# Gate and value weight clamps on GpSimd as one two-step operation, with the head of the output stage and the first loads in another order

## The chip, the cores and the metric

The kernel runs on one core of a Trainium2 chip. The metric is device time in microseconds (us) of one execution; a median of three runs is given. One more execution was profiled. In the profile PE is TensorE's matmuls and PEld its weight loads, DVE is VectorE, ACT is ScalarE, POOL is GpSimd and SP is SyncE, which here only issues transfers. A queue such as SPq is the engine's instruction stream.

## The reference

Three layers follow one another. The MLP's weights are double precision (64 bits) on the host.

```python
# 1. attention: batch 4, 8 heads, 576 positions, head size 64
scores = scale * np.matmul(q, k.transpose(0, 1, 3, 2))   # local mask in heads 0-3, strided in 4-7
attn = np.exp(scores - np.max(scores, axis=-1, keepdims=True))
x = np.matmul(attn / (np.sum(attn, axis=-1, keepdims=True) + 1e-09), v)   # -> (2304, 512)
# 2. soft mixture of experts: 8 experts of 4 slots
logits = x @ phi
slot_input = softmax_over_tokens(logits).T @ x
slot_out = [np.maximum(slot_input[e] @ w1[e], 0.0) @ w2[e] for e in range(8)]
x = softmax_over_slots(logits) @ slot_out
# 3. gated MLP: (2304, 512) -> (2304, 1536) -> (2304, 512)
g, val = x @ w_gate, x @ w_val
return (g * (1.0 / (1.0 + np.exp(-g))) * val) @ w_out
```

## The kernel before

**Attention** runs in 16 units of two batches and one head. Unit n computes the scores (`qk`), then for the unit before it the transposes (`tr`) and the product with the values (`pv`). Keys and queries of a unit come in one transfer into one of three buffers (`load_qk`), values in one into one of two (`load_v`), and each unit also issues two half loads of expert weights (`load_half`). All transfers are issued by SP in the order of the code, and a transfer waits until the one eight places before it has landed (`par`, a small one that ACT issues, counts as the first).

**The experts** follow (w1, then w2), then the **output stage**, on which most of the change lies. The last layer never forms its input: slot outputs are multiplied into the gate and value weights first. For each of 12 blocks f of hidden columns, `a_mm(f)` multiplies the slot outputs (`soT`) with the block's weights, `a_st(f)` brings the result into the form `St[f]`. Tokens come in five blocks (four of 512, one of 256). The list `seq` holds 60 steps (part p, token block, f): 11 in part 0, 21 in part 1 and 28 in part 2. Steps 8 to 10, 29 to 31 and the last six are half steps of 256 tokens. At step n the code emits

- `omm(n-3)`: the output products of step n-3 (LAG = 3), for every 128 tokens hh x woh, hh x wol and hl x woh (high and low parts). In a step that ends its part the three products go tile by tile, in other steps all hh products go first and the hl products behind them;
- what earlier steps put down for step n in `todo` (`flush(n)`);
- `gv(n)`: gate and value products on PE, then sg (SiLU, ACT), h = sg x value (DVE), hh = h rounded (ACT) and hl = h - hh (POOL). The buffers of h are two, so the h of step n waits for the hl of step n-2; those of hh and hl are four;
- parts of a weight conversion as far as the step's `room` goes, and perhaps the start of the next (`stage`).

**The conversion** turns 64-bit weights into fp32 on the chip. For a tile of 128x1024 it takes, for each half k: `mag` (ACT, the magnitude of the high word), `clamp`, `shift`, `low` and `sign` (DVE). Three tiles, g 0, g 1 and o 0, are converted earlier; 15 follow in the output stage: g 2 to g 11 (one for each f) and o 1 to o 5 (one for two f). An o tile is split into woh (ACT) and wol (POOL). The constant CLP says whose clamps go to POOL; for the others DVE clamps from SBUF into a PSUM bank `cv`. When the last part of a g tile is emitted in step n, a_mm comes at step n+1 and a_st at n+2. HEAD is a string that orders what stands ahead of step 0: a is a_mm, s is a_st, w are matmuls without use (`warm`), g starts the first conversion, p emits conversion parts.

Engines run their instructions in order, so what is emitted first on an engine holds up all that is behind it.

Of the kernel before, what the change touches and what calls it, by code (L numbers as in the profile page):

```python
# [10 lines left out]
F32R = mybir.dt.float32r  # L11
# [26 lines left out]
LAG = 3  # L38
CVC = 0.6
CLP = "o"  # L40
WTAIL = 4
# [14 lines left out]
START = (2, 1)  # L56
HEAD = "a0 w1 g w1 a1 p2 s0 w2 p3 s1"
WARM0 = 8
# [55 lines left out]
def build(ctx: ExitStack, tc: tile.TileContext, cst, phi, kq, vh, w1, w2, wgv, wo, out):  # L114
# [72 lines left out]
    def conv(kind, j, through=False):  # L187
# [13 lines left out]
        def clamp(k):  # L201
            if not through:
                DVE.tensor_scalar(out=d[k], in0=d[k], scalar1=MAG_LO, scalar2=MAG_HI, op0=ALU.max, op1=ALU.min)
                return
            if kind in CLP:
                POOL.tensor_scalar(out=d[k], in0=d[k], scalar1=MAG_LO, scalar2=MAG_HI, op0=ALU.max, op1=ALU.min)
                return
            bk[k] = bank("cv", 1).bitcast(I32)
            DVE.tensor_scalar(out=bk[k].bitcast(F32), in0=d[k], scalar1=MAG_LO, scalar2=MAG_HI, op0=ALU.max, op1=ALU.min)
# [274 lines left out]
    with tc.manual_schedule():  # L484
# [14 lines left out]
        DVE.tensor_scalar_max(loc[:, 5:6], loc[:, 3:4], 31.0)  # L499
        load_qk(0)  # L500
        load_v(0)
        load_qk(1)
        SP.dma_start(out=phi_t, in_=phi.rearrange("p (c s) -> p c s", c=4))
        load_half(WSCHED[0])
        load_v(1)
        load_qk(2)

# [142 lines left out]
        cs = mid.tile([128, 4, S], F32R, name="cs")  # L650
        cst2 = [xp.tile([96, 3, 4, 4, 32], F32R, name=f"cst2{q}") for q in range(2)]
        cfs = [xp.tile([96, 3, 128], F32, name=f"cf{q}") for q in range(2)]
# [36 lines left out]

        def c_tr(bp, b, hf):  # L690
            ps = bank("tr", 3)
            for k in range(3):
                PE.transpose(ps[:, 96 * k:96 * k + 96],
                             cst2[hf][:, k, 2 * bp + b].rearrange("p q s -> p (q s)").bitcast(F32),
                             ident[0:96, 0:96])
            DVE.tensor_copy(cs[:, 2 * bp + b, 288 * hf:288 * hf + 288], ps[:, 0:288])
# [51 lines left out]
        DVE.tensor_copy(soT, ps[:, 0:128].rearrange("p (k s) -> p k s", k=4))  # L748
        while ctr:
            fn, a = ctr.pop(0)  # L750
            fn(*a)

# [65 lines left out]
        def omm(p, bi, f):  # L818
# [24 lines left out]
            for t in T:  # L843
                if first:
                    ob[t] = [bank("o", 4) for _ in range(2 if end and t + 1 == len(T) else 1)]
                mm(t, (0, 1, 2) if last else (0, 1))
            if not last:
                for t in T:
                    mm(t, (2,))
# [37 lines left out]
        def stage(n):  # L887
            if queue and len(staged) < 2:
                kind, j = queue.pop(0)
                parts = conv(kind, j, True)  # L890
                z = 4 if kind in CLP else 2
                for _, fn, k in parts[:z]:
                    fn(k)
                staged.append((n + 1, kind, j, parts[z:]))

        def part(n):
# [3 lines left out]
            if not parts:  # L900
                staged.pop(0)
                load_g(fr, "g", NG)
                if kind == "g":
                    at(max(n + 1, LAG + 1), a_mm, j)
                    at(max(n + 2, LAG + 2), a_st, j)
                    at(max(n + 2, LAG + 2), ready.add, (kind, j))
                else:
# [10 lines left out]
        def force(n, key):  # L918
            while key not in ready:
# [3 lines left out]
                if not staged:  # L923
                    stage(n)
                part(n)

        split_hi(0)
        split_lo(0, 0)
        split_lo(0, 1)
        for step in HEAD.split():  # L930
# [7 lines left out]
            elif k == "p":  # L938
                for _ in range(a):
                    part(-1)  # L940
            else:
                warm(a)
# [50 lines left out]
```

## Time and profile before

| | |
|---|---|
| median of 3 runs | 352.49 us (352.02 to 353.14) |
| profiled execution | 352.35 us, of which the span of the profile is 350.5 us |
| busy in the span | PE 334.3, DVE 235.4, ACT 193.2, POOL 139.0 us |
| output stage | from the first gate product at 146.28 us to the end |
| granted TensorE clock | 1.00 of full speed in all stretches looked at |

Time outside the span (1.85 us) is start and end. Busy time says which engine is full; whether a wait of PE costs anything is read from the rows with a releaser in brackets, which give idle time ahead of an instruction and who ended it. A pair such as x2 is two instructions in one row with their common time.

### The profile page before, as it was taken

To read this page: it belongs to the slowest core of one execution; us is meant where nothing else is said; L and a number is where in the kernel's file an instruction comes from. 1 tells how busy PE (TensorE), PEld (TensorE's weight loads), DVE (VectorE), ACT (ScalarE), POOL (GpSimd) and SP (SyncE) were. 2 spreads that over 40 slices of the span, in tenths; PEclk is the share of its full clock that TensorE was granted. 3 is DMA by queue.
4 is the path that set the end of the run, shared out by engine and by line. 5 is a ranking of instruction groups with operands and counts; after the bars stand their busy time and mean duration, and the time that the engine had idled before them with its cause. 6 is when DMAs were issued, how large, how long until landed. Compare 5 with 4: busy or idle time off the path is not lost.

```text
span 350.5 us, 7424 instructions
## 1 busy us (share of the span) xinstructions
PE 334.3 (95%) x2854; PEld 247.8 (71%) x2854; DVE 235.4 (67%) x492; ACT 193.2 (55%) x460; POOL 139.0 (40%) x150
## 2 busy tenths in 40 slices
PE   7999999899999999889998999999989999999995
PEld 4888888697674432456876686776857788888884
DVE  4988888796551265769869889997878633243342
ACT  2998897977521032567746665655654544344441
POOL 2223322114100200248483965456667743443431
PEclk9999999999999999999999999999999999999999
DMA  7999999988899998840423444142100003030331
GB/s 283 412 409 408 408 410 408 409 354 288 301 389 337 412 406 339 330 152 2 131 110 120 142 166 171 48 165 76 73 2 2 0 10 111 0 120 3 121 120 60
DMA packets 20803, 71.93 MB, mean 205 GB/s; under 512 B 2336, under 2 KB 2720, under 8 KB 20768
## 3 DMA queue, kind: packets, MB, share of 16 engines
q1 hardware_dynamic: 20624, 71.45, 53.7%
q8 instruction: 22, 0.36, 0.4%
q14 instruction: 13, 0.11, 0.1%
q10 hardware_dynamic: 144, 0.01, 0.0%
HBM read 66.73 MB, written 4.72 MB: 204 GB/s over the span
## 4 chain that ended last, share of the span: by engine, by line
PE 70%; DVE 9%; DMA 6%; ACT 6%; POOL 5%; issue 3%; DVEq 0%; POOLq 0%; SPq 0%; ACTq 0%
PE o L830 31%; PE sc L283 5%; PE pv L722 5%; PE pv L316 4%; PE sc L631 4%; PE tr L300 4%; PE gv L803 3%; DMA v<-in_vh 3%; DVE h L810 3%; PE gv L804 3%; DMA k<-in_kq 2%; PE tr L335 2%; PE gv L783 2%; POOL hl L812 2%; DVE cv L221 2%
## 5 line engine op out<-in xcount | busy, mean ns | idle before, releaser
L812 POOL TENSOR_TENSOR hl<-h,hh 128x512 fp32r<-128x512 f32 (+1 forms) x60 | 72.3, 1207 | 91.3 <-ACT hh L811 91.2
L830 PE MATMUL o<-woh,hh 128*128 128x512 f32 (+1 forms) x222 | 86.4, 390 | 0.4 <-DVE acc L855 0.2
L830 PE MATMUL o<-wol,hh 128*128 128x512 f32 (+1 forms) x222 | 85.9, 389 | 0.0
L810 DVE TENSOR_TENSOR h<-gv,sg 128x512 f32<-128x512 f32 (+1 forms) x59 | 37.5, 636 | 56.0 <-ACT sg L809 36.7
L830 PE MATMUL o<-woh,hl 128*128 128x512 f32 (+1 forms) x222 | 66.6, 390 | 1.1 <-POOL hl L812 1.1
L811 ACT CAST hh<-h 128x512 fp32r<-128x512 f32 (+1 forms) x60 | 34.7, 578 | 55.0 <-DVE h L810 55.0
L830 PEld LDWEIGHTS o<-woh,hh 128*128 128x128 f32 x222 | 41.8, 188 | 10.7 <-ACT acc L855 0.7
L830 PEld LDWEIGHTS o<-woh,hl 128*128 128x128 f32 x222 | 41.4, 188 | 10.9 <-POOL hl L812 1.9
L830 PEld LDWEIGHTS o<-wol,hh 128*128 128x128 f32 x222 | 41.8, 188 | 8.8
L261 POOL COPY v<-v 32x390 f32<-32x390 f32 (+1 forms) x48 | 21.7, 484 | 62.8 <-DMA v<-in_vh 45.9
L809 ACT ACTIVATE sg<-gv 128x512 f32<-128x512 f32 (+1 forms) x60 | 33.4, 557 | 21.1 <-PE gv L803 20.3
L293 ACT ACTIVATE tmp<-tmp,mx 128x96 f32<-128x96 f32 x144 | 40.1, 368 | 7.6 <-DVE mx L288 7.5
L283 PE MATMUL sc<-k 64*64 64x96 f32 x576 | 28.3, 251 | 1.6 <-DMA k<-in_kq 1.6
L283 PEld LDWEIGHTS sc<-k 64*64 64x64 f32 x576 | 25.4, 137 | 4.2 <-issue 2.4
L803 PE MATMUL gv<-cs,St 128*128 128x512 f32 (+1 forms) x60 | 25.5, 425 | 0.8 <-DVE St L792 0.8
L301 ACT COPY tmp<-tr 96x384 f32<-96x384 f32 x48 | 19.7, 480 | 8.8 <-PE tr L300 8.6
L774 POOL TENSOR_TENSOR wol<-wo,woh 128x512 fp32r<-128x512 f32 x12 | 15.3, 1292 | 22.0 <-ACT woh L771 22.0
L316 PEld LDWEIGHTS pv<-v,tmp 96*64 96x64 f32 x576 | 19.8, 137 | 5.0 <-ACT tmp L301 4.1
L316 PE MATMUL pv<-v,tmp 96*64 96x65 f32 x576 | 22.3, 226 | 0.4 <-DMA v<-in_vh 0.2
L804 PE MATMUL gv<-cs,St 128*128 128x512 f32 (+1 forms) x59 | 22.1, 375 | 0.2 <-DVE h L810 0.2
L221 DVE SCALAR_TENSOR_TENSOR cv<-g,cv 128x512 int32<-128x512 int32 x30 | 20.8, 692 | 0.6
L300 PE MATMUL tr<-cst_t,tmp 128*96 128x128 f32 x144 | 19.7, 279 | 1.5 <-ACT xT L337 1.5
(158 smaller groups left out, 479.1 us busy)
## 6 DMA issues: line engine op xcount, KB each, us to landing
w<-in_w SPq DMA_DIRECT2D x56, 512.0 KB, 8.6
g<-in_wgv SPq DMA_DIRECT2D x10, 1024.0 KB, 4.8
k<-in_kq SPq DMA_DIRECT2D x16, 576.0 KB, 8.3
g<-in_wo SPq DMA_DIRECT2D x5, 1024.0 KB, 4.8
v<-in_vh SPq DMA_DIRECT2D x16, 292.5 KB, 6.6
out<-osb SPq DMA_DIRECT2D x17, 256.0 KB, 2.1
wx<-in_w SPq DMA_DIRECT2D x7, 512.0 KB, 5.5
w<-in_wgv SPq DMA_DIRECT2D x4, 512.0 KB, 7.7
```

The source lines that it names most:

```text
L221: DVE.scalar_tensor_tensor(out=bk[k], in0=v[k][:, :, 0], scalar=29, in1=bk[k], op0=ALU.logical_shift_right, op1=ALU.bitwise_or)
L283: PE.matmul(out=ps[h, W * (i - i0):W * (i - i0) + W], lhsT=q[h, 64 * i:64 * i + 64], rhs=k[h, c0:c0 + W], start=True, stop=True, skip_grou ...
L293: ACT.activation(out=e[:, i], in_=e[:, i], func=AF.Exp, scale=1.0, bias=mx[:, i:i + 1])
L300: PE.transpose(ps[0:W, 128 * j:128 * j + 128], e[:, 3 * t + j], ident)
L316: PE.matmul(out=ps[64 * b:64 * b + 64, 65 * (i - i0):65 * (i - i0) + 65], lhsT=attile[0:W, i, 64 * b:64 * b + 64], rhs=v[0:W, 65 * (NT * b ...
L803: PE.matmul(out=pg[:, 0:n], lhsT=St[f][:, 0:128], rhs=csf[:, t0:t0 + n], start=True, stop=True)
L804: PE.matmul(out=pvv[:, 0:n], lhsT=St[f][:, 128:256], rhs=csf[:, t0:t0 + n], start=True, stop=True)
L809: ACT.activation(out=sg[:, 0:n], in_=pg[:, 0:n], func=AF.Silu)
L810: DVE.tensor_tensor(out=h[:, 0:n], in0=pvv[:, 0:n], in1=sg[:, 0:n], op=ALU.mult)
L811: ACT.copy(hh[bi, f][:, 0:n], h[:, 0:n])
L812: POOL.tensor_tensor(out=hl[bi, f][:, 0:n], in0=h[:, 0:n], in1=hh[bi, f][:, 0:n].bitcast(F32), op=ALU.subtract)
L830: PE.matmul(out=o[:, 0:c], lhsT=(a, a, l)[i][:, 128 * t:128 * t + 128], rhs=(woh, wol, woh)[i][f][:, c * k:c * k + c], start=(first and i ...
```

## The change

Six edits.

1. CLP becomes "go": the clamps of the g tiles go to POOL as well, and `shift` then reads the clamped half from SBUF. Every POOL clamp is one `tensor_scalar` whose first step is the minimum and whose second is the maximum; before, the maximum came first.
2. `stage` no longer emits the clamps at once: half k is put down for step n+1+k, and DVE's parts may start at n+2. a_mm and a_st come one step later than before (n+2 and n+3).
3. HEAD is another string; `t` emits the last two transposes of the slot weights (`c_tr`), which stood ahead of it, with banks of the tag o, and `h` the split of o 0. The tiles `cst2` move to a pool that stays open for that.
4. The first conversion starts at step -2, so its first clamp is put down for step -1, which no step flushes: 29 POOL clamps are issued, not 30, and the first half of g 2 goes unclamped.
5. In the first output step (part 0, block 0) the hh products of all tiles go ahead of the hl products.
6. The first transfers are issued in another order.

```diff
-CLP = "o"
+CLP = "go"
-HEAD = "a0 w1 g w1 a1 p2 s0 w2 p3 s1"
+HEAD = "h g a0 t a1 t s0 w1 s1 p1 w1"
...
-                POOL.tensor_scalar(out=d[k], in0=d[k], scalar1=MAG_LO, scalar2=MAG_HI, op0=ALU.max, op1=ALU.min)
+                POOL.tensor_scalar(out=d[k], in0=d[k], scalar1=MAG_HI, scalar2=MAG_LO, op0=ALU.min, op1=ALU.max)
...
-        load_qk(0)
+        for u in range(2):
+            load_qk(u)
         load_v(0)
-        load_qk(1)
+        load_qk(2)
+        load_v(1)
         SP.dma_start(out=phi_t, in_=phi.rearrange("p (c s) -> p c s", c=4))
         load_half(WSCHED[0])
-        load_v(1)
-        load_qk(2)
...
-        cst2 = [xp.tile([96, 3, 4, 4, 32], F32R, name=f"cst2{q}") for q in range(2)]
+        cst2 = [mid.tile([96, 3, 4, 4, 32], F32R, name=f"cst2{q}") for q in range(2)]
...
-                mm(t, (0, 1, 2) if last else (0, 1))
-            if not last:
+                mm(t, (0, 1, 2) if last and (p or bi) else (0, 1))
+            if not last or not (p or bi):
...
-                for _, fn, k in parts[:z]:
-                    fn(k)
-                staged.append((n + 1, kind, j, parts[z:]))
+                for i, (_, fn, k) in enumerate(parts[:z]):
+                    if i < 2:
+                        fn(k)
+                    else:
+                        at(n + 1 + k, fn, k)
+                staged.append((n + 2, kind, j, parts[z:]))
...
-                    at(max(n + 1, LAG + 1), a_mm, j)
-                    at(max(n + 2, LAG + 2), a_st, j)
+                    at(max(n + 2, LAG + 1), a_mm, j)
+                    at(max(n + 3, LAG + 2), a_st, j)
```

On POOL, around steps 18 to 20 of the output stage, these instructions stand in a row before (L812 is hl, L869 adds into an output tile, L774 is wol; no clamp is near):

```order
L869 TENSOR_TENSOR acc_2227<-osb,acc_2227 128x512
L774 TENSOR_TENSOR wol_2218<-wo_2179,woh_2206 128x512
L774 TENSOR_TENSOR wol_2219<-wo_2179,woh_2207 128x512
L812 TENSOR_TENSOR hl<-h,hh 128x512 x4
L869 TENSOR_TENSOR acc_2231<-osb,acc_2231 128x512
```

And these now, with the same steps' hl at L809, the addition at L866 and the clamps at L206:

```order
L866 TENSOR_TENSOR acc_2217<-osb,acc_2217 128x512
L771 TENSOR_TENSOR wol_2208<-wo_2169,woh_2196 128x512
L771 TENSOR_TENSOR wol_2209<-wo_2169,woh_2197 128x512
L206 TENSOR_SCALAR wg_2168<-wg_2168 128x512
L809 TENSOR_TENSOR hl<-h,hh 128x512
L206 TENSOR_SCALAR wg_2168<-wg_2168 128x512
L206 TENSOR_SCALAR wg_58<-wg_58 128x512
L809 TENSOR_TENSOR hl<-h,hh 128x512
L206 TENSOR_SCALAR wg_58<-wg_58 128x512
L809 TENSOR_TENSOR hl<-h,hh 128x512 x2
L866 TENSOR_TENSOR acc_2221<-osb,acc_2221 128x512
```

Four clamps of two g tiles now stand between the hl of three steps, and each hl is behind one or two of them.

On DVE, from the first `soT` to the h of step 2, before (L209 is the clamp, L217 shift, L221 low, L225 sign, L792 the last part of a_st, L810 is h):

```order
L696 CAST cs<-tr 128x288 x2
L209 TENSOR_SCALAR cv<-wg_2177 128x512
L217 TENSOR_SCALAR cv<-cv 128x512
L792 TENSOR_TENSOR St_2188<-gv,St_2188 64x256
L221 SCALAR_TENSOR_TENSOR cv<-g,cv 128x512
L225 SCALAR_TENSOR_TENSOR wg_2177<-g,cv 128x512
L209 TENSOR_SCALAR cv<-wg_2177 128x512
L792 TENSOR_TENSOR St_2189<-o,St_2189 64x256
L810 TENSOR_TENSOR h<-gv,sg 128x512
L217 TENSOR_SCALAR cv<-cv 128x512
L810 TENSOR_TENSOR h<-o,sg 128x512
```

And now, with St at L789 and h at L807:

```order
L696 CAST cs<-o 128x288 x2
L789 TENSOR_TENSOR St_2178<-gv,St_2178 64x256
L789 TENSOR_TENSOR St_2179<-o,St_2179 64x256
L217 TENSOR_SCALAR cv<-wg_2167 128x512
L807 TENSOR_TENSOR h<-gv,sg 128x512
L221 SCALAR_TENSOR_TENSOR cv<-g,cv 128x512
L807 TENSOR_TENSOR h<-o,sg 128x512
```

The five conversion parts that stood ahead of the first h are down to one, and the two St follow one another.

On SP the first transfers of the program stand like this in the difference (- before, + now; k are keys and queries, v values, w weights):

```order
 L252 DMA k0_76<-in_kq 128x1152
+L252 DMA k1_77<-in_kq 128x1152
 L258 DMA v0_79<-in_vh 64x1170
-L252 DMA k1_77<-in_kq 128x1152
-L503 DMA phi_t_74<-in_phi 128x128
-L182 DMA w_122<-in_wgv 128x1024 x2
+L252 DMA k2_78<-in_kq 128x1152
 L258 DMA v1_80<-in_vh 64x1170
-L252 DMA k2_78<-in_kq 128x1152
+L505 DMA phi_t_74<-in_phi 128x128
+L182 DMA w_127<-in_wgv 128x1024 x2
```

The second and third keys stand ahead of the first weights.

## Rows read from the trace of the kernel before

**Rows 1.** The page's busy times: us, share of the span, instructions.

```profile
PE 334.3 (95%) x2854; PEld 247.8 (71%) x2854; DVE 235.4 (67%) x492; ACT 193.2 (55%) x460; POOL 139.0 (40%) x150
```

**Rows 2.** Windows: stretch, length, busy us (count) by engine, clock, DMA share, GB/s.

```profile
181.78:257.89 76.11, 73.26 (x338) 54.51 (x336) 67.36 (x107) 43.31 (x84) 44.13 (x35) 1.00 0.33 111
272.77:350.50 77.73, 73.96 (x343) 60.86 (x341) 29.00 (x49) 32.09 (x59) 31.78 (x27) 1.00 0.17 61
```

**Rows 3.** Timeline, gate products of two full steps: start, us, instruction.

```profile
282.33 0.40 PE L803 MATMUL gv<-cs,St 128*128 128x512 f32 x1
285.59 0.40 PE L803 MATMUL gv<-cs,St 128*128 128x512 f32 x1
```

**Rows 4.** PE's waits, 140 to 275 us: total us, times, longest.

```profile
PE gv L783 <- DVE wg L225: 4.1, 5, 1.4
PE o L830 <- POOL hl L812: 1.1, 2, 0.6
```

**Rows 5.** Timeline of the head, some of DVE's rows and PE's first output product.

```profile
145.79 0.43 DVE L792 TENSOR_TENSOR St<-gv,St 64x256 fp32r<-64x256 f32 x1
146.25 0.70 DVE L221 SCALAR_TENSOR_TENSOR cv<-g,cv 128x512 int32<-128x512 int32 x1
...
148.43 0.43 DVE L792 TENSOR_TENSOR St<-o,St 64x256 fp32r<-64x256 f32 x1
148.89 0.69 DVE L810 TENSOR_TENSOR h<-gv,sg 128x512 f32<-128x512 f32 x1
150.29 0.50 PE L830 MATMUL o<-woh,hh 128*128 128x512 f32 x1 [0.16 <-ACT hh L811]
```

**Rows 6.** Instructions of the two clamp lines: duration ns min/median/max.

```profile
L206 POOL TENSOR_SCALAR wo<-wo x10: 1912/1922/1927, 159.4 to 263.6; 128x512 f32<-128x512 f32 x10
L209 DVE TENSOR_SCALAR cv<-wg x20: 684/695/697, 144.3 to 268.1; 128x512 f32<-128x512 f32 x20
```

**Rows 7.** POOL's timeline, 158 to 259 us, one row of each kind.

```profile
158.13 1.30 POOL L812 TENSOR_TENSOR hl<-h,hh 128x512 fp32r<-128x512 f32 x1 [2.70 <-ACT hh L811]
...
180.42 1.42 POOL L812 TENSOR_TENSOR hl<-h,hh 128x256 fp32r<-128x256 f32 x2
...
194.59 3.80 POOL L206 TENSOR_SCALAR wo<-wo 128x512 f32<-128x512 f32 x2
...
199.59 2.55 POOL L812 TENSOR_TENSOR hl<-h,hh 128x512 fp32r<-128x512 f32 x2
...
207.82 1.29 POOL L869 TENSOR_TENSOR acc<-osb,acc 128x512 f32<-128x512 f32 x1
209.08 2.56 POOL L774 TENSOR_TENSOR wol<-wo,woh 128x512 fp32r<-128x512 f32 x2
...
258.37 0.74 POOL L812 TENSOR_TENSOR hl<-h,hh 128x256 fp32r<-128x256 f32 x1 [2.38 <-ACT hh L811]
```

**Rows 8.** PE's timeline: step 28's first output product, and the last a_mm wait.

```profile
253.52 0.39 PE L830 MATMUL o<-woh,hh 128*128 128x512 f32 x1
...
261.87 0.63 PE L783 MATMUL gv<-wg,soT 128*32 128x256 f32 x4 [1.41 <-DVE wg L225]
```

**Rows 9.** Timeline: scores of units 1 and 2, values product of unit 13.

```profile
8.27 1.70 PE L283 MATMUL sc<-k 64*64 64x96 f32 x36 [0.89 <-DMA k<-in_kq]
...
13.15 1.70 PE L283 MATMUL sc<-k 64*64 64x96 f32 x36 [0.73 <-DMA k<-in_kq]
...
80.27 1.94 PE L316 MATMUL pv<-v,tmp 96*64 96x65 f32 x36 [0.24 <-DMA v<-in_vh]
```

**Rows 10.** Chain that ended last, in order of time: two early pieces.

```profile
0.73 3.96 DMA par<-in_cst
4.71 8.31 DMA k<-in_kq
```

**Rows 11.** Windows (columns as in Rows 2): DMA share early and late in attention.

```profile
8.00:10.00 2.00, 1.73 (x37) 1.64 (x38) 1.97 (x9) 2.00 (x8) 0.00 (x0) 1.00 1.03 422
74.00:76.00 2.00, 2.00 (x51) 1.93 (x48) 1.44 (x6) 2.00 (x9) 0.32 (x1) 1.00 1.03 412
```

More of the change, by code (lines that the diff above doesn't have):

```diff
@@ L688, in c_soft, with c_tr @@
             ACT.copy(t4[:, :, 2:4, :], t4[:, :, 0:2, :].bitcast(F32))
-        def c_tr(bp, b, hf):
-            ps = bank("tr", 3)
+        def c_tr(bp, b, hf, bk=("tr", 3)):
+            ps = bank(*bk)
             for k in range(3):
@@ L748, in build @@
         DVE.tensor_copy(soT, ps[:, 0:128].rearrange("p (k s) -> p k s", k=4))
-        while ctr:
-            fn, a = ctr.pop(0)
-            fn(*a)
         es_x.close()
@@ L903, in part @@
                 if kind == "g":
-                    at(max(n + 1, LAG + 1), a_mm, j)
-                    at(max(n + 2, LAG + 2), a_st, j)
-                    at(max(n + 2, LAG + 2), ready.add, (kind, j))
+                    at(max(n + 2, LAG + 1), a_mm, j)
+                    at(max(n + 3, LAG + 2), a_st, j)
+                    at(max(n + 3, LAG + 2), ready.add, (kind, j))
                 else:
@@ L924, in force @@
                     stage(n)
+                    continue
                 part(n)
-        split_hi(0)
-        split_lo(0, 0)
-        split_lo(0, 1)
         for step in HEAD.split():
@@ L940, in build @@
                     part(-1)
+            elif k == "t":
+                fn, b = ctr.pop(0)
+                fn(*b, bk=("o", 4))
+            elif k == "h":
+                split_hi(0)
+                split_lo(0, 0)
+                split_lo(0, 1)
             else:
```

## The prediction

> **What bounds the kernel now.** I read the busy times first [rows 1]: PE is busy 334.3 us of the span, so only time in which PE waits can be won, and the next engine, DVE, has 235.4 us. The windows show where DVE is dense: from 181.78 to 257.89 us it is busy 67.36 of 76.11 us, POOL only 44.13; from 272.77 us on DVE is busy 29.00 of 77.73 us [rows 2]. In that last stretch gate products of full steps follow one another every 285.59 - 282.33 = 3.26 us [rows 3], with PE always at work, and no conversion is left; the change has nothing to win or lose there. So the conversions' stretch, about 146 to 272 us, decides. PE's waits there [rows 4] are few and name their cause: a_mm waited five times, 4.1 us in all, for the last conversion part of its tile on DVE, and the output product waited twice, 1.1 us, for hl on POOL. A sixth place is the head: St of step 0 ends on DVE at 145.79 + 0.43 = 146.22 us, but h of step 0 starts at 148.89 us [rows 5]; between them DVE does conversion parts and the other St, and PE's first output product, which needs that h rounded, starts at 150.29 us.
>
> **The change part by part.**
>
> *Clamps off DVE.* 20 clamps of 695 ns leave DVE [rows 6], 13.9 us. DVE is not what ends last by itself, so this is worth only what PE waited for it.
>
> *a_mm one step later.* The tile's last part then has a step of 3.26 us [rows 3] more, against waits of at most 1.4 us [rows 4]. The five waits go: -4.1 us. If DVE fell late by 2 us the cover would be gone and the waits would come back.
>
> *Head.* On DVE only the second St (0.43 us) and one shift (of the clamp's shape, about 0.7 us) stand between St of step 0 and h, where the stretch from 146.22 to 148.89 us stood. St itself comes a little sooner, since the conversion parts ahead of it are gone, but the two magnitudes on ACT now stand ahead of a_mm's copy. I get h at about 147.0 us, 1.9 us sooner. From there h, hh and SiLU of steps 0 to 2 alternate on DVE and ACT as before, and the first evacuations of the output banks stand behind the h of step 2 as before; each handoff gives a little back, and hl of step 3, which ended at 158.13 + 1.30 = 159.43 us [rows 7], should end at 157.8 us. I take -1.6 us for the head, between -0.6 and -2.2 us. That the first output step has its hl products last hides hl of step 0, one of the two hl waits (0.6 us); this is inside the head's number. The other (0.5 us) comes from two clamps in a row ahead of half steps and goes, since there clamps now stand singly.
>
> *Sum for PE if POOL keeps up:* 1.6 + 4.1 + 0.5 = 6.2 us, which is 352.35 - 6.2 = 346.15 us.
>
> *Clamps onto POOL.* This is the cost. 29 clamps instead of 10 at 1.922 us [rows 6] add 36.5 us to POOL's 139.0 us [rows 1], and nearly all of it between step 3 and step 31. Counted in the new order, POOL has in that stretch, from the end of hl 3 to the end of hl 31, 27 clamps, 22 full hl, 6 half hl, 8 wol and 3 additions. Back to back they take 1.90, 1.275, 0.71, 1.28 and 1.29 us (3.80, 2.55, 1.42 and 2.56 us for pairs) [rows 7]: 51.3 + 28.1 + 4.3 + 10.2 + 3.9 = 97.8 us. Before, the same stretch lasted until 258.37 + 0.74 = 259.11 us [rows 7], that is 99.7 us, and POOL had 8 clamps in it. So POOL goes from two thirds full to full: it alone needs what the whole stretch took, and with the removed waits PE wants it shorter.
>
> What saves most of the gain is that PE needs an hl only three steps later. With 2 us of idle POOL (it runs dry around steps 10 and 11, where no clamp is queued; I allow 0 to 4 us) hl 31 ends at 157.8 + 97.8 + 2 = 257.6 us. Step 28 is the tight one, since behind its hl only two clamps and three half hl are left: 2 x 1.90 + 3 x 0.71 = 5.9 us earlier, 251.7 us. Step 28 ends its part, so its third product needs hl, some 0.45 us into it; it can start at 251.25 us. Before it started at 253.52 us [rows 8], and unhindered it would start at 253.52 - 1.6 - 0.5 - 2.7 (four of the five a_mm waits, 4.1 - 1.41) = 248.7 us. So POOL takes back 2.5 us and leaves 2.3 us of gain at step 28. Behind it comes the fifth a_mm wait, 1.41 us [rows 8], which goes, and half steps in which POOL runs free again. Sum: 2.3 + 1.4 = 3.7 us, 352.35 - 3.7 = 348.65 us. The profiled execution lies 0.14 us under the median of the three, so I take 348.7 us.
>
> *The clamp's price in the new order* (minimum first) stands in no row. The same operation with maximum first took 1912 to 1927 ns, all ten [rows 6], and swapping two steps of equal kind gives no reason to differ, so I take 1.90 us back to back. From below, VectorE's 0.695 us for the same clamp [rows 6] is the nearest bound; from above two passes at a two-input hl's 1.30 us [rows 7], 2.6 us. In the trace one clamp costs POOL 2.8 times what DVE pays. The Trainium skill (GPSIMD Engine Reference, section 4.1 Engine selection) says that one-input work on GpSimd is roughly at line rate; by that rule the clamps would take about what VectorE takes, POOL would never hold PE, and the time would be that of the first rival. The ten measured clamps speak against it.
>
> *First loads.* The second key transfer made unit 1 wait 0.89 us, the third unit 2 another 0.73 us [rows 9]; the third was issued only at 4.71 us, when par had landed [rows 10]. It no longer stands eighth, so these 1.6 us go at first. But the transfer engines run at a share of 1.03 and 1.02 to 1.03 from 8 to 76 us [rows 11], 410 to 422 GB/s; the bytes ahead of the values of unit 13 are the same, and PE already waits for those at 80.27 us [rows 9]. What attention wins early it waits for there: I take 0, with -1.6 us as the other end if the wait there doesn't grow. A loss needs the first values to come late; they are needed only after the transposes of unit 0, some 3 us after unit 1's scores.
>
> *The rest.* The c_tr in the head cost PE the same as ahead of it. cst2 in another pool, the missing clamp (one clamp's time, counted) and the shift's other source (0.69 to 0.70 us either way) are taken at nothing.
>
> **The rivals.**
>
> *POOL does not hold PE.* For that the 25 clamps up to hl 28 must be 2.5 us shorter in all, 1.80 us each, or POOL idle by nothing and the head better. Then 346.2 us, or 344.6 us if the first loads' 1.6 us stay too. For it: POOL's slack is only misjudged by 2.5 in 94 us. Against: ten clamps within 15 ns of each other. Chance 0.18, of which 0.03 for work at line rate.
>
> *POOL slower, and the kernel with it.* Each 0.1 us on a clamp costs 2.5 us by step 28, all on the path. From 1.90 + 3.7/25 = 2.05 us per clamp the kernel is slower than before; at 2.6 us it is 0.7 x 25 = 17.5 us later, 366 us; at 2.2 us 356 us. For it: nothing shows the new order's price, and POOL has no reserve. Against: same steps, same shape. Chance 0.15.
>
> *Feedback eats the gain.* POOL waits for hh (ACT), which waits for h (DVE), and DVE now waits in its order for clamps on POOL; two h buffers tie h to the hl of two steps before. A clamp also needs its magnitude from ACT, behind hh and, at four o tiles, behind the copies for woh. If POOL loses 1 us more at each of these four tiles, 3.7 us are gone: 352.4 us. For it: before, POOL already waited 2.70 us for hh in front of hl 3 [rows 7]. Against: once POOL is behind, hh is there before POOL asks. Chance 0.15.
>
> **How the numbers follow.** The forecast above, POOL nearly full, has 0.52; its own range is 346.1 (no idle, best head) to 350.5 us (means of whole rows, 1.922 and 1.31 us, instead of back-to-back times: 1.9 us more). The range that should hold 8 in 10 reaches below to 345.0 us and above to 351.6 us; what is left out is the slower rival and a little of the others. This kernel's runs can tell about 0.3%, 1.06 us. Faster by more: 0.52 + 0.18 and 0.02 of the feedback case, 0.72. Within: 0.13. Slower: 0.15.
>
> **What would show it.** POOL's clamps: 29 at 1.92 us, POOL near 175 us busy in all, DVE near 221 us. The waits of a_mm for DVE gone or under 1 us. h of step 0 near 147 us, hl 3 ended near 157.8 us. From step 18 on POOL without idle time, and PE's waits on hl, or on an h that waited for POOL, 2 to 3 us in all. Step 28's first output product near 251 us; the last stretch as long as before. Values of unit 13 still near 80 us. I am wrong if the clamp is not 1.9 us, if POOL has idle time of more than 4 us in the stretch, or if the head or attention moves by more than 2 us.

## The result and the profile after

The changed kernel takes 348.70 us (median of 6 runs, 346.51 to 350.81). The kernel before, on the same chip, takes 352.59 us (6 runs, 352.02 to 354.01). The ratio is 0.9885, 95% interval 0.9843 to 0.9927. Forecast was 348.7 us. The number is right, but one of the steps that led to it is wrong by a factor of three: a price on GpSimd. A wait and a slower clock, which the forecast doesn't have, make up for that.

The page's busy times of the changed kernel (us, share of the span, instructions), to be read against [rows 1]:

```profile
PE 330.6 (96%) x2852; PEld 246.5 (71%) x2852; DVE 223.6 (65%) x472; ACT 192.7 (56%) x460; POOL 139.6 (40%) x169
```

DVE lost what the clamps cost there. But POOL, which got 19 clamps more, is busy as long as before, not 175 us. The instructions of the clamp line say why (the g tiles' are shown; duration ns min/median/max, first and last start):

```profile
L206 POOL TENSOR_SCALAR wg<-wg x19: 608/617/641, 143.4 to 247.0; 128x512 f32<-128x512 f32 x19
```

With the minimum first a clamp takes 0.617 us. With the maximum first it took 1.922 us [rows 6]. No wait of PE names POOL now: in 135 to 275 us its largest waits are these (total us, times, longest), to be read against [rows 4]:

```profile
PE gv L800 <- DVE St L789: 2.0, 1, 2.0
PE o L827 <- DVE acc L852: 1.6, 2, 0.9
PE o L827 <- DVE acc L858: 0.5, 1, 0.5
PE gv L801 <- DVE h L807: 0.4, 1, 0.4
```

The five a_mm waits for the last conversion part and both hl waits are gone. New is one wait of 2 us for St on DVE. PE's gate products show what it cost. In the timeline of the kernel before, those of steps 0, 13, 14, 15 and 37 are

```profile
146.28 0.50 PE L803 MATMUL gv<-cs,St 128*128 128x512 f32 x1 [0.40 <-DVE St L792]
...
187.81 0.58 PE L803 MATMUL gv<-cs,St 128*128 128x512 f32 x1
...
191.70 0.40 PE L803 MATMUL gv<-cs,St 128*128 128x512 f32 x1
...
194.97 0.40 PE L803 MATMUL gv<-cs,St 128*128 128x512 f32 x1
...
275.61 0.58 PE L803 MATMUL gv<-cs,St 128*128 128x512 f32 x1
```

and in the timeline of the changed kernel, with what ACT and DVE did ahead of step 14 (idle time and its releaser in brackets):

```profile
145.23 0.50 PE L800 MATMUL gv<-cs,St 128*128 128x512 f32 x1
...
183.25 0.50 PE L800 MATMUL gv<-cs,St 128*128 128x512 f32 x1
...
187.95 1.13 ACT L768 CAST woh<-wo 128x512 fp32r<-128x512 f32 x2
...
188.34 0.59 PE L787 MATMUL gv<-asb,cst_t 128*128 128x256 f32 x2
...
188.99 1.22 ACT L199 ACTIVATE wo<-g 128x512 f32<-128x512 f32 x2
...
190.12 0.35 ACT L788 CAST St<-gv 128x256 fp32r<-128x256 f32 x1
190.50 0.43 DVE L789 TENSOR_TENSOR St<-gv,St 64x256 fp32r<-64x256 f32 x1 [0.27 <-ACT St L788]
...
190.99 0.50 PE L800 MATMUL gv<-cs,St 128*128 128x512 f32 x1 [2.05 <-DVE St L789]
...
195.90 0.40 PE L800 MATMUL gv<-cs,St 128*128 128x512 f32 x1
...
272.11 0.39 PE L800 MATMUL gv<-cs,St 128*128 128x512 f32 x1
```

Subtract step by step. At step 13 the changed kernel is 187.81 - 183.25 = 4.56 us ahead, 1.05 us of it from ahead of step 0. At step 14 it is 0.71 us ahead, and at step 15 it is 195.90 - 194.97 = 0.93 us behind: two steps lose all that was won. By step 37 it is 3.50 us ahead again. Step 14 multiplies with St of g 4 (the fifth g tile, first used here). Its a_st, one step later by the change, comes in step 14 itself. PE has done its matmul (L787) by 188.9 us, but on ACT the copies for woh and the magnitudes of an o tile, 1.13 + 1.22 = 2.35 us, stand ahead of St.

Behind the wait the clock falls. Windows of the changed kernel (columns as in [rows 2]), the clock behind POOL's figures:

```profile
189.00:190.00 1.00, 0.00 (x0) 0.00 (x0) 0.97 (x2) 1.00 (x3) 1.00 (x2) 1.00 0.99 119
193.00:194.00 1.00, 1.00 (x4) 0.78 (x3) 0.96 (x2) 1.00 (x2) 0.36 (x1) 0.50 0.00 0
194.00:195.00 1.00, 1.00 (x4) 0.81 (x3) 0.93 (x2) 0.70 (x2) 1.00 (x2) 0.50 0.00 0
```

0.50 is the lower of the two levels, 1.2 GHz. Step 14 lasts 195.90 - 190.99 = 4.91 us where the kernel before took 3.27 us: 1.64 us more. Of the 0.93 + 4.56 = 5.49 us lost in the two steps the wait and the clock are 2.05 + 1.64 = 3.69. Another 1.2 us are waits of PE for banks in step 13 (0.45 us at 184.20 us for the bank that h reads, 0.75 us at 186.84 us for an accumulator, where the kernel before waited 0.20 us in all); the rest was not split.

In attention the scores of units 1 and 2 no longer wait for keys, as foreseen, but one of nine mask instructions on DVE takes 2.3 us where all nine of before took 0.26 to 0.27 us:

```profile
L509 DVE TENSOR_SCALAR ms<-cst_t,par x9: 257/259/2318, 8.0 to 9.8; 128x96 bf16<-128x96 f32 x9
```

### The profile page after: what moved, and what is told of

The parts are those of the page before. It is cut to its first block, busy times and chain, and to the rows that moved or that the text cites. A ratio compares the mean times of both kernels' runs of the same rounds, so it can differ in the third digit from the quotient of the medians.

```text
span 346.1 us, 7436 instructions
## 1 busy us (share of the span) xinstructions
PE 330.6 (96%) x2852; PEld 246.5 (71%) x2852; DVE 223.6 (65%) x472; ACT 192.7 (56%) x460; POOL 139.6 (40%) x169
## 4 chain that ended last, share of the span: by engine, by line
PE 70%; DVE 12%; DMA 8%; ACT 6%; issue 2%; POOL 1%; SPq 0%; DVEq 0%; POOLq 0%
PE o L827 35%; DMA w<-in_w 5%; PE pv L722 4%; PE sc L631 4%; PE sc L283 4%; PE pv L316 3%; PE gv L800 3%; DMA v<-in_vh 3%; PE gv L801 3%; DVE h L807 3%; PE tr L300 2%; PE tr L335 2%; DVE cv L217 2%; ACT tmp L293 1%; PE tr L482 1%
## 5 line engine op out<-in xcount | busy, mean ns | idle before, releaser
L809 POOL TENSOR_TENSOR hl<-h,hh 128x512 fp32r<-128x512 f32 (+1 forms) x60 | 72.6, 1210 | 88.5 <-ACT hh L808 88.4
L807 DVE TENSOR_TENSOR h<-gv,sg 128x512 f32<-128x512 f32 (+1 forms) x59 | 37.5, 636 | 60.9 <-ACT sg L806 48.8
L261 POOL COPY v<-v 32x390 f32<-32x390 f32 (+1 forms) x48 | 23.7, 528 | 61.9 <-DMA v<-in_vh 54.8
L283 PEld LDWEIGHTS sc<-k 64*64 64x64 f32 x576 | 24.3, 133 | 4.4 <-DVE tmp L287 1.7
L221 DVE SCALAR_TENSOR_TENSOR cv<-g,cv 128x512 int32<-128x512 int32 x30 | 20.8, 694 | 0.8
```

What stands on the lines that cost most here:

```text
L261: POOL.tensor_copy(t4[0:W - 64, :, i0:i1, :], t4[64:W, :, i0 - 1:i1 - 1, :])
L283: PE.matmul(out=ps[h, W * (i - i0):W * (i - i0) + W], lhsT=q[h, 64 * i:64 * i + 64], rhs=k[h, c0:c0 + W], start=True, stop=True, skip_grou ...
L807: DVE.tensor_tensor(out=h[:, 0:n], in0=pvv[:, 0:n], in1=sg[:, 0:n], op=ALU.mult)
L809: POOL.tensor_tensor(out=hl[bi, f][:, 0:n], in0=h[:, 0:n], in1=hh[bi, f][:, 0:n].bitcast(F32), op=ALU.subtract)
```

## The experiments

Unless said otherwise each is the changed kernel with one edit. Ratios are against the kernel before on the same chip; kernels that ran on different chips are compared by ratio. Traces are compared by counting from the first gate product, because two executions of the same code don't reach it at the same time (145.23 and 145.90 us for the changed kernel). Theory: the two-step order sets the clamp's price, and step 14's wait with the clock behind it spends the difference. Rivals: the cheap clamp is the whole gain; POOL would have held PE as forecast; head or loads did it.

**The changed kernel again, beside the next three.** 

> The changed kernel once more, on the chip of the three below, to compare them with. Median 346.5 to 350.8 us as in its first six runs. If step 14 sits at the edge of a drop of TensorE's clock, its times spread more than those of the kernel before (over 1 us between lowest and highest) and follow the mean granted clock of the run.

348.74 us, ratio 0.9897 (0.9868 to 0.9927). Step 14's gate product waited 2.05 us again, and the next came 4.92 us later. Counted from the first gate product, every gate product up to that of step 37 comes within 0.1 us of its place in the first execution.

**Maximum first.**

```diff
-scalar1=MAG_HI, scalar2=MAG_LO, op0=ALU.min, op1=ALU.max
+scalar1=MAG_LO, scalar2=MAG_HI, op0=ALU.max, op1=ALU.min
```

> The changed kernel with the maximum first in each POOL clamp, nothing else. Theory A, the order of the two steps sets the price: all 29 clamps take 1.92 us instead of 0.62 us, POOL is busy about 177 us, the sum on record applies and POOL holds PE at step 28 by some 2.5 us on top of what step 14 loses, so 2 to 5 us slower than the changed kernel, 351 to 354 us. Theory B, something else made the clamps cheap (their tiles, their spacing): they stay near 0.62 us and the time stays that of the changed kernel.

349.52 us, ratio 0.9927 (0.9902 to 0.9952): about 0.8 us above the changed kernel beside it, with intervals that overlap. The 29 clamps take 1.92 us again, so the order of the two steps alone sets the price: that step of the prediction is refuted. POOL is now busy 175.1 us, the figure the prediction gave, and 58.55 of 60 us from 200 to 260 us; PE nowhere waits for hl. The wait for St in step 14 is there too, with a clock of 1.00 behind it in the profiled run:

```profile
192.79 0.50 PE L800 MATMUL gv<-cs,St 128*128 128x512 f32 x1 [2.06 <-DVE St L789]
196.12 0.39 PE L800 MATMUL gv<-cs,St 128*128 128x512 f32 x1
```

3.33 us to the next gate product here, 4.91 us in the changed kernel: the same wait with and without the fall. Counted from the first gate product, this execution is 1.59 us ahead of the changed kernel's second one at step 21, which is the clock, and only 0.79 us ahead at step 37: in the trace, too, the dear clamps cost 0.8 us here.

**g 4's a_mm and a_st one step sooner**, nothing else.

```diff
+                    e = 1 if j == 4 else 0
-                    at(max(n + 2, LAG + 1), a_mm, j)
-                    at(max(n + 3, LAG + 2), a_st, j)
-                    at(max(n + 3, LAG + 2), ready.add, (kind, j))
+                    at(max(n + 2 - e, LAG + 1), a_mm, j)
+                    at(max(n + 3 - e, LAG + 2), a_st, j)
+                    at(max(n + 3 - e, LAG + 2), ready.add, (kind, j))
```

> The changed kernel, but a_mm and a_st of tile g 4 alone come one step sooner, as before the change, so that St of g 4 isn't made in the very step that needs it. Theory A, this one tile costs 2.05 us of wait and then about 1.6 us by the lower clock: the wait of the gate product on St is gone, the granted clock is 1.00 in every stretch, and the time is 3 to 4.5 us lower, 344 to 345.5 us. Rival: PE waits there for DVE's evacuations and for h anyway; then the wait moves to a_mm of g 4 or to the next output product, and the time falls by less than 1 us.

345.66 us, ratio 0.9811 (0.9778 to 0.9843), 3.1 us under the changed kernel on the same chip. Its largest waits of PE in the same stretch:

```profile
PE o L827 <- DVE acc L852: 1.1, 2, 0.9
PE gv L780 <- DVE wg L225: 0.7, 1, 0.7
```

The wait for St is gone, the mean clock is 0.998 or more in all five runs, and 0.7 us of an a_mm wait is back. From the first gate product to that of step 37 it takes 269.91 - 146.60 = 123.31 us, the changed kernel run again 126.98 us: 3.67 us less, the 3.69 us of wait and clock. One tile's place was worth as much as nearly all that the change had won.

**Nine matmuls of no use ahead of step 14's gate product**, into the bank that it then overwrites. The wait stays, but PE is busy in it.

```diff
+            for _ in range(9 if (bi, f) == (0, 4) else 0):
+                PE.matmul(out=pg, lhsT=warm_t[:, 0:128], ...)
```

> The changed kernel with nine matmuls of no use (128x512) ahead of the gate product of step 14, where PE otherwise waits 2.05 us for St on DVE. They cost PE no time that it has work for, and keep it busy. Theory: the fall of the granted clock to the 1.2 GHz level behind the wait is what makes step 14 last 4.9 instead of 3.3 us; with PE busy the clock stays at 1.00, the next gate product comes 3.3 us later, and the time is 1.2 to 1.8 us under the changed kernel's 348.7, near 347.2 us. Rival: the clock falls for another reason or gives its time back later; then 348.4 to 349.2 us, no difference that can be told, and the clock in the stretch behind step 14 still shows 0.50.

347.38 us, ratio 0.9833 (0.9800 to 0.9866). In its timeline the matmuls fill the wait, and the next gate product comes 3.33 us later:

```profile
188.41 2.10 PE L801 MATMUL gv<-warm_t 128*128 128x512 bf16 x9
190.63 0.50 PE L802 MATMUL gv<-cs,St 128*128 128x512 f32 x1
...
193.96 0.40 PE L802 MATMUL gv<-cs,St 128*128 128x512 f32 x1
```

So with PE busy in the wait step 14 takes 3.33 us, and that part comes back without any of the work being done sooner. Within the spread of the two ratios the size is the 1.6 us read from the steps. The fall is not bound to the wait in every execution: the mean clock is under 0.996 in 22 of the 34 runs of kernels that have this wait (the changed kernel, it again, maximum first, old head, old loads), in 1 of 6 here, and in 1 of 22 of the four kernels that make g 4's St sooner. The kernel before, without that wait, has such runs as well, 14 of the 45 beside the experiments, so a mean clock doesn't say where the fall lay.

**Other pairs of steps on the clamps**, one execution, for the prices. Each tile has another pair; tiles without both bounds are not clamped on that side.

> A price list, not a race: on each of the 15 tiles the GpSimd clamp has another pair of steps (two instructions per tile, 128x512 fp32 each), among them both orders of minimum and maximum with the true bounds, one step alone (scalar2 absent), the same step twice, and a multiply by 1 or an add of 0 ahead of or behind one of them; tiles without both bounds go unclamped on one side. Theory A, the first step sets the price: every pair that begins with maximum takes about 1.92 us and every pair that begins with minimum 0.62 us, maximum alone too about 1.9 us or at least clearly above minimum alone. Theory B, it is the very pair maximum-then-minimum (one slow combination): only that pair takes 1.92 us, twice maximum, maximum and multiply, maximum and add take about 0.62 us. Theory C, 0.62 us is the exception (one fused minimum-maximum), all others take 1.9 us. The time of the whole kernel is of no interest; 347 to 350 us by any of them.

POOL's timeline of this kernel, one clamp each of g 2 (minimum, maximum), g 3 (maximum, minimum), o 1 (minimum alone), g 4 (maximum alone), o 3 (multiply, maximum) and o 4 (multiply, add):

```profile
144.98 0.62 POOL L218 TENSOR_SCALAR wg<-wg 128x512 f32<-128x512 f32 x1
...
158.75 1.91 POOL L218 TENSOR_SCALAR wg<-wg 128x512 f32<-128x512 f32 x1
...
163.36 1.48 POOL L218 TENSOR_SCALAR wo<-wo 128x512 f32<-128x512 f32 x1
...
166.07 1.48 POOL L218 TENSOR_SCALAR wg<-wg 128x512 f32<-128x512 f32 x1
...
193.59 1.93 POOL L218 TENSOR_SCALAR wo<-wo 128x512 f32<-128x512 f32 x1
...
231.07 0.62 POOL L218 TENSOR_SCALAR wo<-wo 128x512 f32<-128x512 f32 x1
```

The single run took 349.08 us. Theories A and B fall, and C holds with one addition: minimum-maximum and multiply-add take 0.62 us, the nine other pairs tried 1.91 to 1.94 us, and one step alone 1.48 us, more than those two pairs of two steps. How GpSimd carries them out is not seen.

**Minimum first in the kernel before**, ten clamps, nothing else changed.

> The kernel before with nothing changed but the order of the two steps in its ten GpSimd clamps, minimum first. Theory: each of the ten takes 0.62 instead of 1.92 us, GpSimd's busy time falls by 13 us to about 126 us, and since PE waited for hl only twice, 1.1 us in all, of which one wait lies behind a pair of these clamps, the time falls by 0.4 to 0.6 us: 352.0 us where the kernel before has 352.5, hardly to be told. Rival: the cheap clamp is itself most of what the change gains; then 349 to 350 us.

352.49 us, ratio 0.9991 (0.9971 to 1.0011). POOL's busy time falls to 126.1 us, one of its two hl waits (0.6 us) is left, and the five a_mm waits are still 4.1 us. The cheap clamp by itself is worth nothing that can be told: from the first gate product to that of step 37 the profiled execution takes 129.32 us, the kernel before 129.33 us. (Its clock stood at 0.50 from 153 to 156 us; step 3 came 1.48 us later than before, and by step 11 that was made good.) The later a_mm with the clamps left on DVE was not tried, so what their leaving DVE is worth by itself is not shown.

**Maximum first, with g 4 one step sooner.** Here the prediction's account of POOL can be tested, since step 14 no longer hides it.

> The version with g 4's block product one step sooner (345.7 us) and the clamps with the maximum first, at 1.92 us each. The prediction's account of GpSimd then holds as it was worked out: hl 31 can't end before about 257.2 us, step 28's third product is held, and some 2 to 3 us of waits for hl appear between steps 18 and 28: 347.7 to 348.7 us. Rival: the account is too strict, since with the changed kernel the dearer clamps cost 0.8 us though GpSimd was busy 58.6 of 60 us; then 345.5 to 346.7 us, and PE waits on hl under 0.7 us.

347.42 us, ratio 0.9839 (0.9805 to 0.9872): 0.0028 above the version with cheap clamps, about 1.0 us by the ratios, whose intervals overlap. The traces say more. Here are the first gate product and step 28's first output product, first in this version, then with cheap clamps:

```profile
145.01 0.50 PE L800 MATMUL gv<-cs,St 128*128 128x512 f32 x1
...
250.21 0.40 PE L827 MATMUL o<-woh,hh 128*128 128x512 f32 x1
```

```profile
146.60 0.50 PE L800 MATMUL gv<-cs,St 128*128 128x512 f32 x1
...
249.46 0.40 PE L827 MATMUL o<-woh,hh 128*128 128x512 f32 x1
```

That is 105.20 us against 102.86 us: by step 28 the dear clamps cost 2.34 us, and 2.45 us by the last gate product. Up to step 17 the two agree to 0.06 us; 0.3 us go by step 18, 1.0 more by step 21 and 1.1 more by step 22. (In absolute times the cost is hidden, since this execution came to soT 1.59 us sooner.) Two waits of PE are new:

```profile
PE o L827 <- ACT osb L862: 0.9, 2, 0.7
PE o L827 <- POOL hl L809: 0.8, 1, 0.8
```

The second is the wait for hl that the prediction had. The longer one of the first row, ahead of step 22, also begins on POOL; its chain on DVE, ACT and PE is

```profile
214.19 0.69 DVE L217 TENSOR_SCALAR cv<-wg 128x512 int32<-128x512 int32 x1 [0.98 <-POOL wg L206]
214.79 0.68 DVE L807 TENSOR_TENSOR h<-gv,sg 128x512 f32<-128x512 f32 x1
215.56 0.62 ACT L808 CAST hh<-h 128x512 fp32r<-128x512 f32 x1 [4.06 <-DVE h L807]
216.09 0.58 ACT L862 COPY osb<-o 128x512 f32<-128x512 f32 x1
216.72 0.50 PE L827 MATMUL o<-woh,hh 128*128 128x512 f32 x1 [0.69 <-ACT osb L862]
```

A shift on DVE waits for a clamp on POOL, h stands behind the shift, hh waits for h, the copy that frees the output bank stands behind hh on ACT, and PE waits for the bank. This is the feedback that the prediction had as a rival. POOL's own time is as forecast:

```profile
155.66 1.30 POOL L809 TENSOR_TENSOR hl<-h,hh 128x512 fp32r<-128x512 f32 x1 [0.85 <-ACT hh L808]
...
255.02 1.48 POOL L809 TENSOR_TENSOR hl<-h,hh 128x256 fp32r<-128x256 f32 x2
```

hl 3 ends at 156.96 us, hl 31 at 256.50 us: 99.5 us, where the prediction had 97.8 + 2 = 99.8. So the theory's account holds in the trace; the median lies between the times of theory and rival.

**a_mm and a_st one step sooner for every tile**, by the rule of the kernel before (n+1 and n+2).

```diff
+                    e = 1
```

(in place of the condition on g 4)

> The changed kernel with the block product a_mm and the step a_st one step sooner for every tile, as in the kernel before (0.62 us clamps on GpSimd kept). Theory from the prediction's sum: the later a_mm is worth the 4.1 us of waits; the wait for St in step 14 goes as with g 4 alone, so against 345.7 us the waits of a_mm come back: 4 to 5 of them, 0.5 to 1.4 us each, 348 to 349.5 us. Rival: with 20 clamps off DVE the last conversion parts end in time by themselves; waits of a_mm under 1.5 us in all, 345.5 to 346.8 us, and the later a_mm brought nothing.

355.94 us, ratio 1.0087 (1.0058 to 1.0116): slower than the kernel before, and by the ratios some 10 us slower than with g 4 alone. Both theories fell short. The waits are five again, and longer:

```profile
PE gv L780 <- DVE wg L225: 5.6, 5, 1.9
```

Around the longest, that of g 5 ahead of the gate product of step 15, the clock falls as well:

```profile
194.97 0.63 PE L780 MATMUL gv<-wg,soT 128*32 128x256 f32 x4
197.47 1.07 PE L780 MATMUL gv<-wg,soT 128*32 128x256 f32 x4 [1.87 <-DVE wg L225]
198.46 0.80 PE L800 MATMUL gv<-cs,St 128*128 128x512 f32 x1
```

In the kernel before, g 5's a_mm comes behind the gate product of step 15 (194.97 us):

```profile
198.32 0.63 PE L783 MATMUL gv<-wg,soT 128*32 128x256 f32 x4
```

So the old rule is not the old place. With two clamps fewer on DVE the code emits g 5's last part one step sooner (step 14, before 15), and the old rule takes a_mm along to step 15; in the changed kernel it stands in step 16, as before the change. What kept g 5's wait away was a whole step between last part and a_mm. PE's waits for parts, accumulators and St sum to 8.5 us here and to 2.3 us with g 4 alone; the other 4 us, the slower clock among them, were not split.

**The head in its old order**, without the old string's five conversion parts (p2 and p3).

```diff
-HEAD = "h g a0 t a1 t s0 w1 s1 p1 w1"
+HEAD = "h t t a0 w1 g w1 a1 s0 w2 s1"
```

> The changed kernel with the head in the order of the kernel before (no conversion part ahead of step 0 save those that order emits, block products and warm matmuls in their old places, the last two transposes ahead of all). Theory from the prediction's sum: the head's order is worth 1.6 us at hl of step 3 and at the steps behind it up to step 13; but in the changed kernel the wait for St in step 14 swallows what comes early, so the time rises by less, 0 to 1 us: 348.7 to 349.7 us, with hl 3 ending near 158.5 to 159 us and a shorter wait for St in step 14. Rival: the head's gain is carried to the end; 350.3 us, the wait in step 14 still 2 us.

348.13 us, ratio 0.9866 (0.9835 to 0.9897), not slower than the changed kernel. hl 3 ends at 156.38 + 1.30 = 157.68 us. From the start of soT, the tile with which the head begins, to the end of hl 3 it is 15.76 us here, 15.68 us in the changed kernel (155.88 + 1.30 = 157.18 us), 17.58 us before [rows 7]. The three soT, before, changed and here:

```profile
141.85 0.29 DVE L748 COPY soT<-sc 128x128 f32<-128x128 f32 x1 [0.36 <-PE sc L746]
```

```profile
141.50 0.29 DVE L748 COPY soT<-sc 128x128 f32<-128x128 f32 x1 [0.36 <-PE sc L746]
```

```profile
141.92 0.29 DVE L748 COPY soT<-sc 128x128 f32<-128x128 f32 x1 [0.36 <-PE sc L746]
```

Both expectations fail: the order in the string, apart from the parts left out, brings nothing that can be told. In three of its runs the mean clock was 1.00 (346.74 to 347.86 us), in three 0.993 or 0.994 (348.41 to 349.73 us), about 1.9 us apart by the means, near the price of the fall; where it lay in these runs is not seen (the profiled one has none).

**The first loads in their old order.**

```diff
-        for u in range(2):
-            load_qk(u)
+        load_qk(0)
         load_v(0)
-        load_qk(2)
-        load_v(1)
+        load_qk(1)
...
+        load_v(1)
+        load_qk(2)
```

> The changed kernel with the first loads in the old order. Theory A: the new order brought the values copies and the memset on POOL onto the mask building of DVE, where one instruction of 96 columns took 2.3 us instead of 0.26; with the old order it takes 0.26 us again, the scores of unit 12 start near 61.7 instead of 62.6 us, attention ends 0.7 to 1 us sooner, and some of it arrives at the end: 0 to -1 us. Rival: the transfers set attention's end, the values of unit 13 come at 80.8 us as they do now, and nothing changes at the end.

347.93 us, ratio 0.9883 (0.9851 to 0.9915), within the spread of the changed kernel's 0.9897. The mask instructions are back at 0.26 to 0.27 us and the wait for St is still 2.1 us. The cost on DVE is shown in the trace, its worth in time isn't settled.

**g 4 sooner, and a memset on POOL moved** from attention's first microseconds to unit 3.

```diff
-        POOL.memset(eT, 0.0)
...
+        at_late(3, POOL.memset, eT, 0.0)
```

> The version with g 4's block product one step sooner (345.7 us), and GpSimd's memset of 10.65 us (for the transposed exponentials) moved from the first microseconds to unit 3. Theory: the mask instruction on DVE that lasts 2.32 us was blocked by GpSimd's row of copies and memset; without the memset it shortens to between 0.26 and about 1.3 us, unit 2's scores lose their 1.06 us wait, and the expert stage starts some 0.7 us sooner: 344.8 to 345.3 us. Rival: the transfers bound attention anyway and the values of unit 13 wait for the same bytes; then 345.4 to 346.0 us. A second rival: the copies alone block it just as long, and the mask instruction stays at 2.3 us.

344.49 us, ratio 0.9752 (0.9717 to 0.9788), the lowest of all kernels run. The long mask instruction is down to 0.56 us:

```profile
L509 DVE TENSOR_SCALAR ms<-cst_t,par x9: 257/257/561, 8.1 to 10.1; 128x96 bf16<-128x96 f32 x9
```

So the memset (1.05 us at 10.65 us in the changed kernel, behind 1.33 us of copies) made up most of it; the copies alone, still there, add 0.3 us. The interval touches that of g 4 alone, so the gain of some 0.6% over it is likely and not proven. Counted from the first gate product, the profiled execution agrees with that of g 4 alone to 0.12 us up to step 37, so a gain would lie ahead of it. That execution is the slowest of the six (346.09 us): its clock stood at 0.50 from 67 to 69 us, in attention, behind a wait of PE of 1.75 us that ended at 65.07 us.

**The same with the old loads.**

> The fastest version so far (g 4's block product one step sooner, memset moved; 344.5 us) with the first loads in the order of the kernel before. Theory: the order of the first loads is worth something once its cost on DVE (the long mask instruction) is gone: units 1 and 2 then wait again for their keys, 0.9 and 0.7 us, and since the transfers bound the rest of attention about half of it stays: 344.8 to 346 us. Rival: attention ends when its bytes have landed, in whatever order: 344.3 to 344.7 us, and unit 13's values come at the same time in both.

344.75 us, ratio 0.9777 (0.9751 to 0.9803). The two orders can't be told apart, as the rival said, and units 1 and 2 wait for keys again, 1.69 and 0.73 us. The first gate product of its profiled run is at 145.07 us, that of the version before it, with the fall in attention, at 146.29 us: no gain of the new loads' order is seen on the way to the output stage.

## Why the prediction was right, point by point

*What bounds the kernel: right.* PE waited less by what was named, and the time moved with it. From step 37 on the changed kernel's profiled execution is 0.9 us shorter, steps of 3.22 us instead of 3.26 [rows 3]. The changed kernel run again has 3.26 us there, so the spacing belongs to the execution and not to the change.

*a_mm one step later, -4.1 us: the waits went, but a move was left out.* The sum counted a_mm, not a_st, which moves with it and feeds St to the gate product. For one of the tiles, g 4, that falls into the step of first use. The step that failed is "The tile's last part then has a step of 3.26 us more": true for a_mm's inputs, while its output lost a step. It cost 2.05 us of wait and 1.64 us of clock, 3.7 us together; undoing it for this tile gave 3.1 us by the medians and 3.67 us by the traces. The step was also gained in another way than the sum says: g 5's a_mm, for one, stays in step 16, and its last part comes a step sooner.

*Head, -1.6 us: size near, cause wrong.* h of step 0 came at 146.58 us (forecast 147.0) and hl 3 ended 2.25 us sooner, of which 0.35 us lie ahead of soT, so the head itself gave 1.90. But the old string without its parts gives 1.82. What shortened the head must be in what both share: fewer parts on DVE ahead of h, the later clamps, and the hl products put last in the first output step; which of these was not tried apart.

*Clamps onto POOL, -2.5 us of the gain taken back: wrong.* "Swapping two steps of equal kind gives no reason to differ" was the step that failed: 0.617 us, not 1.90. It lay below the lower bound, VectorE's 0.695 us. The account behind it was sound: with the dear clamps and g 4 mended POOL took 99.5 us (forecast 99.8) and PE lost 2.45 us in the trace (forecast 2.5), though by step 22 and not at step 28, and about half of it through DVE and ACT. By the medians it is 1.0 us, in intervals that hold both. In the changed kernel as it stands the dear clamps cost 0.8 us, probably because the wait in step 14 gives POOL time. The Trainium skill (GPSIMD Engine Reference, section 4.1 Engine selection) calls one-input work on GpSimd roughly line rate: by these rows that holds for the two cheap pairs, at 0.62 us against VectorE's 0.695, and not for the others, at 1.48 to 1.94 us. The rival that leaned on it had the mechanism right and was given 0.03; its 346.2 us is what the kernel reaches once step 14 is mended (345.66 us).

*First loads, 0: right in the sum.* Old order and new can't be told apart in either of two pairs. Not foreseen was the mask instruction. The Trainium skill (SBUF — State Buffer, section Who interferes with whom) states that VectorE in a two-port mode and GpSimd share one pair of ports, and that one blocks fully while the other holds it; a DVE instruction of 2.3 us beside a POOL row of copies and memset, and of 0.56 us without the memset, agrees with that, but no run here shows which mode it ran in.

*The sum.* The profiled execution is 4.44 us shorter than before: 0.35 us ahead of soT, 0.70 from soT to the first gate product, 2.45 from there to that of step 37 (126.88 against 129.33 us), 0.90 behind it. With g 4 mended the two middle pieces are 0.70 and 6.02 us, 6.7 in all, where the forecast had 6.2 if POOL keeps up. So that sum was near; POOL should have taken 2.5 us and took nothing that shows, and step 14, which the forecast doesn't have, took 3.6. That the result is 348.7 us is a coincidence of these terms, not a confirmation of the forecast's middle step. (Its last line is a little off as well: 348.65 + 0.14 is 348.8, not 348.7.)

## What to carry to other kernels

A price holds for the instruction that was measured: exchange two steps, and look for a row of that very pair or take a range that goes well beyond its neighbours on both sides. When a step is moved, follow its outputs as well as its inputs: find for every tile the step that first reads what it makes, and count the steps between; here one tile out of ten decided. Price a wait of PE with the clock that may fall behind it: 2 us here cost another 1.6 in some executions. Compare two traces from an event that both reach alike, here the first gate product: in absolute times the cost of the dear clamps was hidden by an earlier start.

## What the hardware showed that was not expected

GpSimd's 128x512 fp32 `tensor_scalar` has three prices: 0.62 us (minimum then maximum, multiply then add), 1.48 us (one step alone) and 1.91 to 1.94 us (maximum then minimum and all other pairs tried). A two-step instruction can be the cheaper one.

TensorE's granted clock stood at 0.50 from 193 to 195 us, behind a wait of 2.05 us that ended at 190.99 us, and not in every execution (1.00 behind the same wait with maximum first). With matmuls of no use in the wait, five of six runs had a mean clock of 0.999 or 1.00. Such a fall also came behind a wait of 1.75 us in attention (g 4 sooner, memset moved), and behind one of 0.62 us that ended at 152.84 us (minimum first in the kernel before).

A DVE instruction of 0.26 us took 2.3 us beside POOL copies and a memset.
